# Two scalars loaded to one partition and spread by a product of ones, with the opening of the kernel reordered around them

## The chip, the cores and the metric

The kernel runs on one core of a Trainium2 chip. The metric is device time in microseconds of one execution, as the median of several runs. A core has five instruction streams that run beside each other and meet at semaphores: TensorE (PE, matrix products; its weight loads are shown apart as PEld), VectorE (DVE), ScalarE (ACT), GpSimd (POOL) and SyncE (SP, which here only issues DMA transfers). ScalarE can issue transfers too.

## The reference

Sparse attention followed by a feed-forward layer, both in float32. q, k and v have 4 batches, 8 heads, 768 positions and 64 dimensions; `n_global` is 8 and `n_local` is 96, and both come as int64 inputs.

```python
scores = q @ k.T / sqrt(D)
is_global = pos[None, :] < n_global
is_local = (rel >= 0) & (rel < n_local)          # rel = row - column
keep = is_global | is_local
dist = where(is_global & ~is_local, n_local, abs(rel))
scores = where(keep, scores - slopes * dist, -1e9)
a = softmax(scores)
x = (a @ v) in rows of 512                       # 3072 rows
h = x @ w_in                                     # 512 -> 2048
g = where(h > 0, h, exp(min(h, 0)) - 1)
out = g @ w_out                                  # 2048 -> 512
```

The two numbers are read at run time: the masks and distances of the attention depend on them.

## The kernel before, in words

The 3072 rows are worked in 12 groups of 256 rows (two tiles of 128). For each group there are four pairs of heads. A pair loads q and k together in one tile (`qk`, 312 KB) and its values in `v` and `u`; q is scaled (line 447 on ScalarE, 449 on GpSimd, 451 on VectorE), TensorE makes scores `s` (line 472), VectorE adds a table (`far0` for the first tile of a group, `far1` for the second) and takes the minimum (line 460), ScalarE takes the exponential (462), the result is divided by its sum, transposed on TensorE (525, 527), copied from PSUM to `pt` and multiplied with the values (505). The feed-forward products are lines 834 and 860 for the first four groups and 710 and 766 for the later eight. The weights come as float64 in 32 loads of 512 KB (`bits`, line 389), which VectorE, ScalarE and GpSimd turn into a high and a low float32 part (lines 391 to 410).

Nearly all of this is put in order by a planner, `Plan`, written in Python: it simulates the five engines with a cost for each operation, and gives each engine a list. Operations are picked by the earliest possible start and then by a due time; due times are counted from fixed points such as `T0` = 34 us. Three of its numbers describe the start of the program: `BW0` is the time at which transfers begin to flow, and `FREE` says when each engine is first free. They change no instruction, but move what the planner believes of the opening, and so can change which operation goes first anywhere later.

Ahead of the planned list stands `setup`, whose instructions are in the order in which they are written. It first issues the load of the two scalars from ScalarE's queue (`load_scalars`, line 228), to all 128 partitions. GpSimd writes index tables with iota, VectorE makes from them the signed distance `d`, the part of the table that doesn't depend on the scalars, and a small table `g` for the 8 global columns. When the scalars have landed, VectorE puts each together from its two 32-bit words (`scalars`, line 235) and finishes the tables: `d` becomes a mask by `n_local` (363), `g` is made of `n_global` and `n_local` (364, 366), `far0` and `far1` get the mask added (365, 367), and the global columns are put in, in `far0` by VectorE (370) and in `far1` by GpSimd (371). After that GpSimd makes the identity matrix that the transposes need, and sets small constants in the tiles `st`. From then on all engines work through the planned list.

TensorE has no work until the first scores. `warm` (line 1065 and on) fills the time with products of a tile of ones, whose result nobody reads: `COLD` = 8 of them at the start, and later, until the first feed-forward product, as many of 240 ns as the planner sees idle time for. In the trace these are `none<-fill`, line 1070.

Of the kernel before, what the change touches and what calls it, by code (L numbers as in the profile page):

```python
# [8 lines left out]
F32 = mybir.dt.float32  # L9
F32R = mybir.dt.float32r  # L10
I32 = mybir.dt.int32
AF = mybir.ActivationFunctionType
ALU = mybir.AluOpType
# [3 lines left out]
P = 128  # L17
NG = 8
# [8 lines left out]
BIG = float(2 ** 100)  # L27
# [32 lines left out]
class Plan:  # L60
# [3 lines left out]
    LAT = {"PE": 170.0, "ACT": 110.0, "DVE": 90.0, "POOL": 70.0, "SP": 1900.0}  # L64
    BW = 380.0

    BW0 = 2250.0

    FREE = {"PE": 5200.0, "ACT": 3600.0, "DVE": 5300.0, "POOL": 6000.0, "SP": 700.0}

    def __init__(self):
        self.ops = []
# [36 lines left out]
    def order(self, slots):  # L109

        free = {}
        for names in slots.values():
            for s in names:
                free[s] = 0.0
        engines = dict(self.FREE)
        port = 0.0
        bw = self.BW0
        queue = {}
# [109 lines left out]

def load_scalars(nc, pool, src):
    n = src.shape[0]  # L230
    raw = pool.tile([P, n, 2], I32, name="n_raw")
    nc.scalar.dma_start(raw, src.bitcast(I32).rearrange("(o n w) -> o n w", o=1, w=2).broadcast_to([P, n, 2]))
    return raw


def scalars(nc, pool, raw):

    n = raw.shape[1]
    up = pool.tile([P, n], F32, name="n_up")
    nc.vector.scalar_tensor_tensor(up, raw[:, :, 0], 0.0, raw[:, :, 1], ALU.is_lt, ALU.add)  # L240
    val = pool.tile([P, n], F32, name="n_val")
    nc.vector.scalar_tensor_tensor(val, up, float(2 ** 32), raw[:, :, 0], ALU.mult, ALU.add)
    return [val[:, i:i + 1] for i in range(n)]


class Kernel:
# [77 lines left out]
    def setup(self):  # L324

        nc, m = self.nc, self.m
        self.raw = load_scalars(nc, self.c, self.n_in)  # L330
        far0, far1 = self.far0.t, self.far1.t
        t = self.c.tile([P, 1], F32, name="act")
        ii = m.tile([P, LW], I32, tag="io0", name="ii")
        d = m.tile([P, LW], F32, tag="io1", name="d")
        j = self.c.tile([P, NG], I32, name="tabj")
        g = self.c.tile([P, NG], F32, name="tabg")
        after = m.tile([P, LW], F32, tag="io2", name="after")
        halves = ((slice(0, HW), BACKW + 32), (slice(HW, P), BACKW - 32))
        nc.gpsimd.memset(t, 0.0)
        nc.scalar.activation(t, t, AF.Exp)  # L340
        if self.WARM:
            self.fill = m.tile([P, 512], F32R, tag="xh2a", name="fill")
            nc.vector.memset(self.fill.bitcast(F32), 1.0)
            self.none = self.ps.tile([P, 512], F32, tag="h1", name="none")

        for r, at in halves:
            nc.gpsimd.iota(ii[r, :at + NG], pattern=[[-1, at + NG]], base=BACKW, channel_multiplier=1)
            nc.gpsimd.iota(ii[r, at + NG:], pattern=[[-1, LW - at - NG]], base=BACKW - at, channel_multiplier=1)
        nc.gpsimd.iota(j, pattern=[[1, NG]], base=0, channel_multiplier=0)
        nc.vector.tensor_copy(d, ii)  # L350
        nc.vector.tensor_scalar(after, d, 0.0, -BIG, ALU.is_lt, ALU.mult)
        nc.vector.scalar_tensor_tensor(far1, d, -1.0, after, ALU.mult, ALU.add)
        nc.scalar.copy(far0, far1)
        nc.vector.tensor_copy(g, j)
        for h in range(0, self.H, 2):
            nc.gpsimd.memset(self.scale.t[:, h // 2:h // 2 + 1], self.q_scale(h))
        nc.gpsimd.tensor_scalar(self.scale.t[HW:], self.scale.t[HW:], 2.0, 1.0, ALU.mult, ALU.mult)
        for r, at in halves:
            nc.gpsimd.memset(far0[r, :at - 32], -BIG)
            nc.gpsimd.memset(far0[r, at:at + NG], -BIG)  # L360
        self.ng, self.nl = scalars(nc, self.c, self.raw)
        ng, nl = self.ng, self.nl
        nc.vector.tensor_scalar(d, d, nl, -BIG, ALU.is_ge, ALU.mult)
        nc.vector.tensor_scalar(g, g, ng, -BIG, ALU.is_ge, ALU.mult)
        nc.vector.tensor_tensor(far0, far0, d, ALU.add)
        nc.vector.tensor_scalar(g, g, nl, None, ALU.subtract)
        nc.vector.tensor_tensor(far1, far1, d, ALU.add)
        for r, at in halves:
            x = far0[r, at - 32:at - 32 + NG]
            nc.vector.tensor_tensor(x, x, g[r], ALU.max)  # L370
            nc.gpsimd.tensor_copy(far1[r, at:at + NG], g[r])
        make_identity(nc, self.ident.t)
        if self.ON_PE:
            nc.scalar.activation(self.minus1.t, self.ident.t, AF.Copy, scale=-1.0)
        for x in self.sums.values():
            nc.gpsimd.memset(x[:, :, 1], 1e-9)


    def weight(self, which, fc, due, after):
# [608 lines left out]

    SLACK, LATER = 600.0, 3500.0

    GATE, COLD = 900.0, 8
    HINT = 40
    LOADED = 2000.0
    BACK = 3500.0
# [22 lines left out]
    def run(self):  # L1017
        self.consts()
        self.build()
        order = self.plan.order(self.slots())  # L1020
        with self.tc.manual_schedule():
            first = order[0]
            for v in first.allocs:
                v.t = v.make(v.slot)
            first.emit(first.eng)
            self.setup()
            free = self.warm(self.COLD * 240.0, 0.0)
            cold = min(op.n for op in order if op.eng == "PE" and op.allocs and op.allocs[0].cls == "h")
            last = max(i for i, op in enumerate(order) if op.eng == "PE" and op.allocs and op.allocs[0].cls == "s")
            end = max(i for i, op in enumerate(order) if op.eng == "PE")  # L1030

            self.norms = [(op.norm, op.start) for op in order if op.norm is not None and op.norm.eng == "DVE"]
            for i, op in enumerate(order):
                if op is first:
                    continue
                if op.n == cold:
                    self.WARM = False
                if op.eng == "PE" and self.WARM:

                    self.warm(op.start - free, 300.0)  # L1040
                    free = op.start + op.alts[0][1]
                for v in op.allocs:
                    v.t = v.make(v.slot)
                if op.eng == "POOL":
                    self.gate(op)
                op.emit(op.eng)
                if i == last + 40:
                    flags = self.flag()
                if i == last + 80:
                    self.flag_sum(flags)  # L1050
                if i == len(order) - self.HINT:
                    self.tc.mark_branch_hint_location("dense", hint="LikelyTaken", engines=list(mybir.ALL_ENGINES))
                if i == end:
                    flag = self.flagged()
        return flag
# [10 lines left out]
    def warm(self, ns, least):  # L1066

        nc = self.nc
        while self.WARM and ns > least:
            nc.tensor.matmul(self.none, self.fill[:, :P], self.fill, start=True, stop=True)  # L1070
            ns -= 240.0
        return self.plan.FREE["PE"]

# [225 lines left out]
```

## Time and profile before

| what | before |
|---|---|
| median of 3 runs | 644.77 us (644.61 to 646.71) |
| the profiled execution | 645.74 us, of which the span from first to last instruction is 643.9 |
| TensorE busy | 629.8 us, 98% of the span |
| VectorE busy | 495.8 us, 77% |
| ScalarE busy | 414.3 us, 64% |
| GpSimd busy | 196.9 us, 31% |
| mean granted clock of TensorE | 0.994 |
| moved by DMA | 149.82 MB, 233 GB/s |

A busy share is an average over the whole span. Stages differ, so the rows below go by stage. An instruction's row gives its start, its duration, its engine and line, output and input tiles, and in brackets how long the engine was idle before it and what ended that. "Landing" is the time from the issue of a transfer to its completion. The granted clock is 1.00 where TensorE runs at 2.4 GHz and 0.50 where it runs at 1.2 GHz.

### The profile page before, as it was taken

Reading aid. Unit: us, or ns where it says so; the run is one execution under the profiler, and the core shown is the slowest. Engines: PE = TensorE matmul, PEld = TensorE weight load, DVE = VectorE, ACT = ScalarE, POOL = GpSimd, SP = SyncE. Lnnn points to the kernel's source line nnn. Section 1 sums busy time; section 2 is a strip of 40 time slices with the busy share of each in tenths; the row PEclk is TensorE's granted clock in tenths of the full one; section 3 lists DMA queues with packets and bytes.
Section 4 is the critical chain, followed back from the end, with each engine's and each line's share of the span. In section 5 each row is a group of like instructions: output and inputs, shape, how many; then the busy total and the mean of one; then the engine's idle time right before and its main releaser. Section 6 shows DMA issues by size and latency. Waiting matters only on the chain.

```text
span 643.9 us, 19099 instructions
## 1 busy us (share of the span) xinstructions
PE 629.8 (98%) x7032; PEld 581.9 (90%) x7032; DVE 495.8 (77%) x1648; ACT 414.3 (64%) x1206; POOL 196.9 (31%) x493
## 2 busy tenths in 40 slices
PE   7989999999999999999999999999999999999995
PEld 5768888888888889999999999999999999999995
DVE  6989889888888886777767777786686776875654
ACT  6999777677554656666666576566566566555452
POOL 3546555656456662121121111112022112110000
PEclk9989999999999999999999999999999999999998
DMA  8979824322266799897879788898898898884542
GB/s 310 379 271 406 330 85 113 94 88 85 66 213 240 235 292 305 262 283 238 259 242 294 254 253 270 271 262 240 271 268 274 282 246 269 251 244 147 181 149 85
DMA packets 131171, 149.82 MB, mean 233 GB/s; under 512 B 63616, under 2 KB 82816, under 8 KB 131072
## 3 DMA queue, kind: packets, MB, share of 16 engines
q1 hardware_dynamic: 130928, 148.54, 72.6%
q8 instruction: 57, 0.93, 0.6%
q14 instruction: 42, 0.34, 0.2%
q10 hardware_dynamic: 144, 0.00, 0.0%
HBM read 117.57 MB, written 30.93 MB: 231 GB/s over the span
## 4 chain that ended last, share of the span: by engine, by line
PE 90%; DVE 3%; DMA 2%; ACT 2%; issue 1%; POOL 1%; SPq 0%; DVEq 0%; POOLq 0%; ACTq 0%
PE h L710 27%; PE o L766 24%; PE o L860 14%; PE h L834 14%; PE s L608 5%; PE s L472 4%; PE pv L505 2%; PE t L525 1%; DMA dd<-tr 1%; DMA pt<-dd 1%; DMA n_raw<-in_n_dram 1%; PE t L527 1%; DVE pr L460 1%; DVE pt L305 0%; ACT pr L462 0%
## 5 line engine op out<-in xcount | busy, mean ns | idle before, releaser
L710 PE MATMUL h<-xh,w 128*128 128x256 f32 x1024 | 142.1, 280 | 0.0
L710 PEld LDWEIGHTS h<-xh,w 128*128 128x128 f32 x1024 | 129.8, 188 | 1.9 <-issue 1.0
L720 DVE SCALAR_TENSOR_TENSOR gg<-e,h 128x256 f32<-128x256 f32 x128 | 53.3, 416 | 76.8 <-ACT e L719 76.2
L578 POOL TENSOR_SCALAR pr<-pr,st 128x168 f32<-128x168 f32 x144 | 63.0, 437 | 154.3 <-DVE st L480 141.8
L462 ACT ACTIVATE pr<-pr,nmax 128x168 f32<-128x168 f32 x192 | 82.0, 428 | 14.7 <-DVE nmax L460 12.9
L834 PEld LDWEIGHTS h<-xh,w 128*128 128x128 f32 x512 | 76.8, 188 | 10.8 <-DVE gl L311 0.8
L718 ACT ACTIVATE e<-h 128x256 f32<-128x256 f32 x128 | 48.6, 380 | 57.1 <-PE h L710 56.9
L834 PE MATMUL h<-xh,w 128*128 128x256 f32 x512 | 82.0, 283 | 0.1
L710 PE MATMUL h<-xl,w 128*128 128x256 f32 x512 | 81.8, 281 | 0.0
L860 PE MATMUL o<-w,gh 128*128 128x512 f32 x256 | 81.5, 400 | 0.0
L710 PEld LDWEIGHTS h<-xl,w 128*128 128x128 f32 x512 | 69.3, 188 | 1.9 <-issue 1.7
L460 DVE CUSTOM_DVE_ANT_0 pr<-s,far 128x168 f32<-128x168 f32 x192 | 53.4, 324 | 13.2 <-ACT xh L303 11.2
L311 POOL TENSOR_TENSOR w<-g,w 128x256 fp32r<-128x256 f32 x64 | 50.7, 813 | 38.2 <-ACT w L303 29.9
L303 ACT CAST sh<-sum 128x512 fp32r<-128x512 f32 x64 | 39.8, 622 | 31.3 <-DVE sum L734 31.3
L583 DVE STREAM_TRANSPOSE tr<-pr 128x192 f32<-128x192 f32 x144 | 50.4, 364 | 8.3 <-POOL pr L578 7.9
L719 ACT ACTIVATE e<-e 128x256 f32<-128x256 f32 x128 | 53.4, 417 | 3.6
L766 PE MATMUL o<-mix,sh 128*128 128x256 f32 x256 | 51.0, 281 | 0.0
L860 PEld LDWEIGHTS o<-w,gh 128*128 128x128 f32 x256 | 43.0, 188 | 7.6 <-issue 1.7
L311 DVE TENSOR_TENSOR sl<-sum,sh 128x512 fp32r<-128x512 f32 x64 | 44.4, 694 | 5.2 <-ACT sh L303 5.2
L766 PE MATMUL o<-w,sh 128*128 128x256 f32 x256 | 48.2, 280 | 0.0
L449 POOL TENSOR_SCALAR qk<-qk,scale 128x256 f32<-128x256 f32 x13 | 7.5, 578 | 129.9 <-DMA qk<-in_qkv_dram 84.9
L303 ACT CAST rh<-gg 128x384 fp32r<-128x384 f32 x64 | 32.8, 513 | 19.4 <-DVE gg L720 18.7
(131 smaller groups left out, 1416.7 us busy)
## 6 DMA issues: line engine op xcount, KB each, us to landing
mix<-mixed SPq DMA_DIRECT2D x192, 256.0 KB, 4.5
qk<-in_qkv_dram SPq DMA_DIRECT2D x48, 312.0 KB, 4.2
v<-in_qkv_dram SPq DMA_DIRECT2D x36, 384.0 KB, 4.8
dd<-tr SPq DMA_DIRECT2D x36, 384.0 KB, 4.4
pt<-dd SPq DMA_DIRECT2D x72, 192.0 KB, 3.9
bits<-in_w_in_dram SPq DMA_DIRECT2D x16, 512.0 KB, 7.1
bits<-in_w_out_dram SPq DMA_DIRECT2D x16, 512.0 KB, 9.5
mixed<-mix SPq DMA_DIRECT2D x32, 256.0 KB, 3.8
```

What stands on the lines that cost most here:

```text
L303: self.nc.scalar.copy(out, x)
L311: self.on(e).tensor_tensor(out, x, y, ALU.subtract)
L460: first = p.add((("DVE", 85 + 1.042 * LW, False),), lambda e: nc.vector.tensor_tensor_reduce(x(), s.t[:, i, :LW], tab, -(2.0 ** -(h + 1)), ...
L462: p.add(act(LW, extra=200), lambda e: nc.scalar.activation(x(), x(), AF.Exp, bias=nm, scale=-1.0, accum_out=st.t[:, n, 0:1]), [pr], [pr, s ...
L578: nc.gpsimd.tensor_scalar(pr.t[:, :LW], pr.t[:, :LW], st.t[:, n, 3:4], 1.0, ALU.mult, ALU.mult)
L583: nc.vector.transpose(tr.t[:, :, i, j], pr.t.rearrange("p (b r) -> p b r", r=32))
L710: nc.tensor.matmul(h.t, w1.t[:, s, cc * P:(cc + 1) * P], self.chunk(x, cc), start=n == 0 and s == HI and cc == 0, stop=n == 1 and cc == se ...
L719: p.add(act(W), lambda e: nc.scalar.activation(ex.t, ex.t, AF.Exp, scale=-1.0), [ex], [ex], d - 8000)
L720: p.add(dve(W), lambda e: nc.vector.scalar_tensor_tensor(gs(), ex.t, -1.0, h.t, ALU.add, ALU.max), [h, ex], [g], d - 8000)
L766: nc.tensor.matmul(acc[bank].t[:, half], a, b.t[:, LO if t == 1 else HI, x], start=j == 0 and t == 0 and n in first, stop=j == self.NFC // ...
L834: nc.tensor.matmul(h.t, w1.t[:, s, cc * P:(cc + 1) * P], self.chunk(x, cc), start=n == 0 and cc == 0, stop=n == 2 and cc == self.NCC - 1)
L860: nc.tensor.matmul(o.t[:, :at.stop - at.start], g.t[:, i * P:(i + 1) * P], w2.t[:, s, at], start=fc == f0 and n == 0 and s == HI, stop=fc ...
```

## The change

- The scalars are loaded to one partition instead of 128. VectorE puts them together there, TensorE multiplies them with a row of 128 ones, which gives every partition a copy in PSUM, and VectorE copies that to SBUF.
- The cast of `g` and its two steps with the scalars move from VectorE to GpSimd, the two steps now with a second operation that changes nothing (add 0).
- `make_identity` moves ahead of the table steps that need the scalars; the constants in `st` are now set before GpSimd's copies into `far1`; on VectorE the mask is added to `far1` after the global columns are put into `far0`.
- Of the opening products three stand before the product that spreads the scalars and two behind it, instead of eight in a row.
- The planner's starting numbers become smaller: transfers flow from 1.2 us on instead of 2.25, and the engines are free from 4.1 (TensorE), 3.0 (ScalarE), 4.4 (VectorE) and 4.6 us (GpSimd) instead of 5.2, 3.6, 5.3 and 6.0.

```diff
-    BW0 = 2250.0
-    FREE = {"PE": 5200.0, "ACT": 3600.0, "DVE": 5300.0, "POOL": 6000.0, "SP": 700.0}
+    BW0 = 1200.0
+    FREE = {"PE": 4100.0, "ACT": 3000.0, "DVE": 4400.0, "POOL": 4600.0, "SP": 700.0}
...
 def load_scalars(nc, pool, src):
-    raw = pool.tile([P, n, 2], I32, name="n_raw")
-    nc.scalar.dma_start(raw, src.bitcast(I32).rearrange("(o n w) -> o n w", o=1, w=2).broadcast_to([P, n, 2]))
+    raw = pool.tile([1, n, 2], I32, name="n_raw")
+    nc.scalar.dma_start(raw, src.bitcast(I32).rearrange("(o n w) -> o n w", o=1, w=2))
...
+    up = pool.tile([1, n], F32, name="n_up")
     nc.vector.scalar_tensor_tensor(up, raw[:, :, 0], 0.0, raw[:, :, 1], ALU.is_lt, ALU.add)
+    one = pool.tile([1, n], F32, name="n_one")
+    nc.vector.scalar_tensor_tensor(one, up, float(2 ** 32), raw[:, :, 0], ALU.mult, ALU.add)
+    all_ = psum.tile([P, n], F32, tag="h0", name="n_all")
+    nc.tensor.matmul(all_, ones[0:1, :P], one, start=True, stop=True)
     val = pool.tile([P, n], F32, name="n_val")
-    nc.vector.scalar_tensor_tensor(val, up, float(2 ** 32), raw[:, :, 0], ALU.mult, ALU.add)
+    nc.vector.tensor_copy(val, all_)
...
+        nc.vector.memset(ones, 1.0)
...
-        nc.vector.tensor_copy(g, j)
...
+        nc.gpsimd.tensor_copy(g, j)
...
+        make_identity(nc, self.ident.t)
+        self.warm(self.COLD[0] * 240.0, 0.0)
+        self.ng, self.nl = scalars(nc, self.c, self.raw, ones, self.ps)
+        nc.gpsimd.tensor_scalar(g, g, ng, -BIG, ALU.is_ge, ALU.mult)
+        nc.gpsimd.tensor_scalar(g, g, nl, 0.0, ALU.subtract, ALU.add)
         nc.vector.tensor_scalar(d, d, nl, -BIG, ALU.is_ge, ALU.mult)
-        nc.vector.tensor_scalar(g, g, ng, -BIG, ALU.is_ge, ALU.mult)
         nc.vector.tensor_tensor(far0, far0, d, ALU.add)
-        nc.vector.tensor_scalar(g, g, nl, None, ALU.subtract)
-        nc.vector.tensor_tensor(far1, far1, d, ALU.add)
         for r, at in halves:
             x = far0[r, at - 32:at - 32 + NG]
             nc.vector.tensor_tensor(x, x, g[r], ALU.max)
-            nc.gpsimd.tensor_copy(far1[r, at:at + NG], g[r])
-        make_identity(nc, self.ident.t)
+        nc.vector.tensor_tensor(far1, far1, d, ALU.add)
         for x in self.sums.values():
             nc.gpsimd.memset(x[:, :, 1], 1e-9)
+        for r, at in halves:
+            nc.gpsimd.tensor_copy(far1[r, at:at + NG], g[r])
...
-    GATE, COLD = 900.0, 8
+    GATE, COLD = 900.0, (3, 2)
...
-            free = self.warm(self.COLD * 240.0, 0.0)
+            free = self.warm(self.COLD[1] * 240.0, 0.0)
```

## Rows read from the trace of the kernel before

**Rows 1.** Busy time by stage: stretch, length, each engine's us (instructions), clock, DMA, GB/s
```profile
core 0: us, PE busy (x) PEld busy (x) DVE busy (x) ACT busy (x) POOL busy (x), PEclk, DMA share, GB/s
12.00:28.00 16.00, 15.31 (x224) 11.21 (x223) 15.26 (x66) 14.42 (x50) 7.09 (x14) 1.00 1.03 400
44.00:68.00 24.00, 22.59 (x279) 18.06 (x279) 22.86 (x77) 22.31 (x75) 15.87 (x22) 1.00 1.01 396
100.00:620.00 520.00, 519.64 (x5894) 490.96 (x5893) 398.24 (x1316) 323.86 (x933) 142.25 (x382) 1.00 0.74 227
```
**Rows 2.** The opening in order of time: start, duration, engine, line, operation, tiles, idle before
```profile
0.82 0.41 ACTq L232 DMA_DIRECT2D n_raw<-in_n_dram  x1
0.86 0.39 SPq L427 DMA_DIRECT2D qk<-in_qkv_dram  x1
1.54 3.59 PE L1070 MATMUL none<-fill 128*128 128x512 f32 x8 [1.54 <-DVE fill L343]
4.83 0.16 DVE L240 SCALAR_TENSOR_TENSOR n_up<-n_raw 128x2 f32<-128x2 int32 x1 [1.96 <-DMA n_raw<-in_n_dram]
5.24 0.51 ACT L447 ACTIVATE qk<-qk,scale 128x256 f32<-128x256 f32 x1 [2.09 <-DMA qk<-in_qkv_dram]
5.80 0.80 PE L472 MATMUL s<-qk 64*64 64x168 f32 x16 [0.67 <-ACT qk L447]
6.29 0.35 DVE L370 TENSOR_TENSOR far<-far,tabg 64x8 f32<-64x8 f32 x2
6.44 0.41 POOL L371 COPY far<-tabg 64x8 f32<-64x8 f32 x2 [2.83 <-DVE far L367]
6.80 0.33 DVE L460 CUSTOM_DVE_ANT_0 pr<-s,far 128x168 f32<-128x168 f32 x1
7.67 0.49 POOL L449 TENSOR_SCALAR qk<-qk,scale 128x256 f32<-128x256 f32 x1
8.21 0.80 PE L472 MATMUL s<-qk 64*64 64x168 f32 x16 [0.48 <-POOL qk L449]
8.76 0.48 POOL L449 TENSOR_SCALAR qk<-qk,scale 128x256 f32<-128x256 f32 x1 [0.60 <-DMA qk<-in_qkv_dram]
```
**Rows 3.** Transfers: packets by queue from 2.0 to 4.75, and issues (KB each, us to landing)
```profile
q1 hardware_dynamic: 185, 0.41, 54.8%
q10 hardware_dynamic: 132, 0.00, 2.2%
...
n_raw<-in_n_dram ACTq DMA_DIRECT2D x1, 2.0 KB, 4.0
qk<-in_qkv_dram SPq DMA_DIRECT2D x1, 312.0 KB, 4.3
...
qk<-in_qkv_dram SPq DMA_DIRECT2D x1, 312.0 KB, 5.0
```
**Rows 4.** Stages again: the transfers' first start, and two later starts from rest
```profile
2.13:4.50 2.37, 2.37 (x7) 1.88 (x6) 0.68 (x3) 0.94 (x3) 0.56 (x5) 1.00 0.56 137
39.00:40.50 1.50, 1.50 (x24) 1.39 (x23) 1.35 (x4) 1.19 (x4) 0.28 (x1) 1.00 0.89 219
69.75:71.50 1.75, 1.75 (x36) 1.56 (x36) 1.17 (x4) 0.99 (x2) 0.85 (x2) 1.00 0.86 194
```
**Rows 5.** Two opening products (ns min/median/max, first and last start); a stage
```profile
L1070 PE MATMUL none<-fill x2: 434/531/628, 4.3 to 4.7; 128*128 128x512 f32 x2
...
8.20:11.20 3.00, 2.99 (x36) 2.10 (x36) 1.69 (x13) 2.68 (x13) 1.64 (x4) 1.00 1.04 414
```
**Rows 6.** The dip of the clock: TensorE in order of time, and the stage
```profile
35.56 0.69 PE L525 MATMUL t<-ident,pr 128*128 128x128 f32 x2 [1.26 <-ACT pt L303]
36.60 1.40 PE L472 MATMUL s<-qk 64*64 64x168 f32 x16
...
35.50:38.60 3.10, 3.04 (x32) 2.10 (x34) 1.41 (x10) 2.32 (x10) 1.82 (x4) 0.50 0.39 147
```

More of the change, by code (lines that the diff above doesn't have):

```diff
@@ L230, in load_scalars, with scalars @@
     n = src.shape[0]
-    raw = pool.tile([P, n, 2], I32, name="n_raw")
-    nc.scalar.dma_start(raw, src.bitcast(I32).rearrange("(o n w) -> o n w", o=1, w=2).broadcast_to([P, n, 2]))
+    raw = pool.tile([1, n, 2], I32, name="n_raw")
+    nc.scalar.dma_start(raw, src.bitcast(I32).rearrange("(o n w) -> o n w", o=1, w=2))
     return raw
-def scalars(nc, pool, raw):
+def scalars(nc, pool, raw, ones, psum):
     n = raw.shape[1]
-    up = pool.tile([P, n], F32, name="n_up")
+    up = pool.tile([1, n], F32, name="n_up")
     nc.vector.scalar_tensor_tensor(up, raw[:, :, 0], 0.0, raw[:, :, 1], ALU.is_lt, ALU.add)
+    one = pool.tile([1, n], F32, name="n_one")
+    nc.vector.scalar_tensor_tensor(one, up, float(2 ** 32), raw[:, :, 0], ALU.mult, ALU.add)
+    all_ = psum.tile([P, n], F32, tag="h0", name="n_all")
+    nc.tensor.matmul(all_, ones[0:1, :P], one, start=True, stop=True)
     val = pool.tile([P, n], F32, name="n_val")
-    nc.vector.scalar_tensor_tensor(val, up, float(2 ** 32), raw[:, :, 0], ALU.mult, ALU.add)
+    nc.vector.tensor_copy(val, all_)
     return [val[:, i:i + 1] for i in range(n)]
@@ L337, in setup @@
         after = m.tile([P, LW], F32, tag="io2", name="after")
+        ones = self.c.tile([1, P], F32, name="ones")
         halves = ((slice(0, HW), BACKW + 32), (slice(HW, P), BACKW - 32))
@@ L340, in setup @@
         nc.scalar.activation(t, t, AF.Exp)
[L341 to L344, printed above, removed]
+        self.fill = m.tile([P, 512], F32R, tag="xh2a", name="fill")
+        nc.vector.memset(self.fill.bitcast(F32), 1.0)
+        self.none = self.ps.tile([P, 512], F32, tag="h1", name="none")
         for r, at in halves:
@@ L360, in setup @@
             nc.gpsimd.memset(far0[r, at:at + NG], -BIG)
-        self.ng, self.nl = scalars(nc, self.c, self.raw)
+        make_identity(nc, self.ident.t)
+        if self.ON_PE:
+            nc.scalar.activation(self.minus1.t, self.ident.t, AF.Copy, scale=-1.0)
+        self.warm(self.COLD[0] * 240.0, 0.0)
+        self.ng, self.nl = scalars(nc, self.c, self.raw, ones, self.ps)
         ng, nl = self.ng, self.nl
+        nc.gpsimd.tensor_scalar(g, g, ng, -BIG, ALU.is_ge, ALU.mult)
+        nc.gpsimd.tensor_scalar(g, g, nl, 0.0, ALU.subtract, ALU.add)
         nc.vector.tensor_scalar(d, d, nl, -BIG, ALU.is_ge, ALU.mult)
-        nc.vector.tensor_scalar(g, g, ng, -BIG, ALU.is_ge, ALU.mult)
         nc.vector.tensor_tensor(far0, far0, d, ALU.add)
-        nc.vector.tensor_scalar(g, g, nl, None, ALU.subtract)
-        nc.vector.tensor_tensor(far1, far1, d, ALU.add)
         for r, at in halves:
@@ L370, in setup @@
             nc.vector.tensor_tensor(x, x, g[r], ALU.max)
-            nc.gpsimd.tensor_copy(far1[r, at:at + NG], g[r])
-        make_identity(nc, self.ident.t)
-        if self.ON_PE:
-            nc.scalar.activation(self.minus1.t, self.ident.t, AF.Copy, scale=-1.0)
+        nc.vector.tensor_tensor(far1, far1, d, ALU.add)
         for x in self.sums.values():
             nc.gpsimd.memset(x[:, :, 1], 1e-9)
+        for r, at in halves:
+            nc.gpsimd.tensor_copy(far1[r, at:at + NG], g[r])
     def weight(self, which, fc, due, after):
```

## The prediction, made before the changed kernel ran

> **What bounds the kernel now.** I read the page's busy shares first (TensorE 629.8 us of a span of 643.9), then a table of stages, then the opening in order of time. The stages [rows 1] say where a saved microsecond counts. From 100 to 620 us TensorE is busy 519.64 of 520: that stretch is bound by TensorE, the edit adds and removes nothing in it, so it comes earlier or later as a block, and the stores at the end with it. The result is decided by when TensorE gets through the opening, before about 100 us. There, from 12 to 28 us, everything is nearly full: VectorE 15.26 of 16, ScalarE 14.42, DMA share 1.03 at 400 GB/s; from 44 to 68 it is the same (22.86 and 22.31 of 24, 396 GB/s). Such a stretch can't be hurried by one engine alone; but if loads and softmaxes both start earlier by the same amount, it is shifted whole.
>
> The opening in order of time [rows 2] has two chains. One is the scalars: issued at 0.82, used by VectorE at 4.83 after an idle of 1.96 us; then the table steps, GpSimd's copies into far1 (it was idle 2.83 us before them), its identity matrix and st memsets, its scaling of the second qk at 7.67, score products at 8.21. The other is the first qk load: issued at 0.86, scaled by ScalarE at 5.24 after an idle of 2.09 us, score products at 5.80, and the first softmax step at 6.80, which the tables and not the scores hold back: those have been there since 6.6. The landing times are 4.0 us for the scalars and 4.3 for qk [rows 3].
>
> **The scalar load.** Before, it is 2 KB to 128 partitions; its queue shows 132 packets between 2.0 and 4.75 us beside 185 of the main queue [rows 3]. From 2.13 to 4.5 us the engines moved 137 GB/s x 2.37 us = 325 KB at a share of only 0.56 [rows 4]. Twice later the transfers start from rest with no such load beside them: 219 GB/s over the first 1.5 us at 39.0, 194 over 1.75 us at 69.75. The same 325 KB take 1.48 or 1.68 us at these rates, 0.89 or 0.69 us less than 2.37. I read that as small and large packets being fed to the same engines in turn. Bounds for what the removal gives the first qk: 0 (every start from rest is slow, and the small packets cost nothing) and 1.56 us (325 KB at the 400 GB/s of the full stretch take 0.81). I take 0.9, the restart at 39.0, the nearer one in size of transfer: a qk load again. The Trainium skill (DMA: Bandwidth & Descriptors, "HWDGE ordering") says that SP's and ScalarE's queues each have one ring on the same 16 engines and no descriptor generator of their own. By that rule the small packets do cost the large ones, and the term stands near 0.9; two independent queues would put it at 0. The shares of rows 3 and 4 side with the rule without proving it.
>
> The scalars' own landing lies between 2.1 us (the stretch of rows 4 begins at 2.13 with the first packet of the main queue, 1.27 us after its issue, and a single small packet has nothing behind it) and 4.8 as now. VectorE comes to the first scalar step only when its earlier steps are done, now at 4.83 - 1.96 = 2.87; the cast of g leaves it there and a memset of ones comes in, so about 2.9. I take "landed by then"; one packet is far from 132.
>
> **The spread.** Two one-partition steps (0.16 each, as n_up now), a product with two columns (between nothing and the 0.63 of an opening product at the low clock [rows 5]; I take 0.4), a copy from PSUM (0.16 again), three hand-overs of 0.05, like the one from ScalarE's end at 5.75 to the scores at 5.80: 2.9 + 0.32 + 0.4 + 0.16 + 0.15 = 3.9 us for n_val, against 5.2 now (4.83 and two steps). If the scalars land no earlier, it is 5.9, 0.7 late. From n_val the table steps now run until 6.64, 1.4 us; two of them, the steps on g, go to GpSimd (0.2 each, as its copies of the same size) and run beside d and far0: about 1.2 is left, so tables at 5.1.
>
> **GpSimd.** Identity and st memsets fill 0.82 us between the far1 copies (end 6.85) and the scaling at 7.67. Both go ahead of the copies, the identity ahead of the wait for n_val too, into the idle of 2.83 us, and are hidden; if that idle is gone, they cost their 0.82 again. Behind the new wait for n_val stand the g steps, memsets, far1 copies (0.41) and all scalings of qk. Copies end at 5.1 + 0.05 + 0.41 = 5.6. The second qk was issued at 2.24 and took 5.0 us to land [rows 3]: 7.24 now, 6.35 with 0.9 off. So the load, not GpSimd, is then last: second scores at 6.35 + 0.49 + 0.05 = 6.9 instead of 8.21. The third qk, for which GpSimd waits already (8.76), comes 0.9 earlier.
>
> **The opening products.** Eight in a row become three, the small product, and two. With the first qk at 4.35, ScalarE's 0.51 and a hand-over put the scores at 4.9. Eight take 3.59 us, so three end near 2.9; the spread's product runs by 3.7 and two more end by 4.6: they don't hold up the scores, and cost 0 on the path. If the scalars land at 4.8, they do, to about 6.5.
>
> **Sum.** First scores 5.80 to 4.9, second 1.3 earlier, third qk 0.9 earlier: the smallest, 0.9, goes into the full stretch at 12 us, since DMA is full there as well. The profiled execution took 645.74 (the span and 1.84 around it), 0.97 above the median: 645.74 - 0.9 = 644.8 for it, and 644.77 - 0.9 = 643.9 for the median. The planner's lower start times (BW0 by 1.05 us, TensorE by 1.1, GpSimd by 1.4) also change which operation is issued next, and how many planned products fill gaps. No row prices that; I take 0, with ends of 1.5 us either way, the largest single disturbance of the opening, which comes next.
>
> **Rivals.** (1) *A dip of the clock goes too.* At 34.3 TensorE sits idle 1.26 us for a ScalarE copy, and from 35.5 to 38.6 the granted clock is 0.50, 1.2 GHz [rows 6]: 16 score products take 1.40 us instead of 0.80. TensorE is busy 3.04 of these 3.1 us, work for 1.5 at the full clock. The dip hangs on one wait, and the order changes; but ScalarE, for which it waits, stays nearly full, so a wait can come back anywhere. Time 643.9 - 1.5 = 642.4.
>
> (2) *The earlier start is not earlier.* If the slow start is the transfers' own, qk keeps its 4.3 us, only the tables gain, and the full DMA stretch takes that back: 644.8. The restart at 69.75, with 0.69, speaks half for it.
>
> (3) *Slower, by the clock.* Of the opening products the one at 4.3 takes 0.63 us and the last, at 4.7, 0.43 [rows 5]: the clock rises from 1.2 to 2.4 GHz there, 3.2 us after the first of them at 1.54, with unbroken products before it, and ahead of the first scores. After the edit there are gaps near 3.0 and 3.5. If the level stays low through the first scores, the stretch from 8.2 to 11.2, now 2.99 of 3 us busy [rows 5] and on the chain, takes longer: twice as long at worst, +3.0; if the clock rises 3.2 us after the scores begin, about +1.2 for two groups of scores (0.60 each). With 0.9 off that is 645.1 to 646.9; I take 645.9. It decides if the first 16 score products last 1.4 us rather than 0.8. For it speaks the pause; against it, that each pause is under 0.6 us. The Trainium skill (TensorE: Matmul & The Clock Gate, "What's actually happening") says that the low level is the state of rest and that activity releases it. The opening rows agree, and by that rule cutting eight products to five is a risk that the diff does not show.
>
> **How the numbers follow.** Forecast 643.9 with 0.45 (own range 643.2 to 644.6: the shift between 0.2 and 1.56); dip gone, 642.4, with 0.27; no shift, 644.8, with 0.13; clock, 645.9, with 0.15. About 0.3%, 1.9 us, is what a measurement here can tell from no change, so faster is under 642.84 and slower over 646.7. Faster: most of the dip case (0.22) and 0.08 of the forecast with a luckier order, 0.30. Slower: a third of the clock case and an unlucky order, 0.08. Same: 0.62. The range 641.8 to 646.1 leaves out dip cases with an extra gain and the worse half of the clock case, about 0.15.
>
> **What would show it.** Right: VectorE has no wait for the scalars; ScalarE's first scaling near 4.35, first scores near 4.9, first softmax step near 5.5 (now 6.80), second scores near 6.9, loads of the first 28 us about 0.9 earlier; and the stretch from 100 to 620 us unchanged but early. Wrong: the first scaling still at 5.2; score groups of 1.4 us in the opening; another stretch at 0.50, or none, between 28 and 68 us; a gain at 12 us that is gone at 100.

## The result and the profile after

| | before | after |
|---|---|---|
| median, runs side by side (21 each) | 645.61 us (644.61 to 648.38) | 648.76 us (646.58 to 656.66) |
| ratio after/before, 95% interval | | 1.0057 [1.0043, 1.0071] |
| the profiled execution | 645.74, span 643.9 | 649.79, span 648.0 |
| TensorE busy, granted clock | 629.8 us, 0.994 | 632.7 us, 0.997 |

The changed kernel is slower: by 3.1 us between the medians, by 0.57% or 3.7 us in the ratio, where 0.9 us of gain was forecast and 646.1 was the upper end. (The execution of 656.66 us, at a granted clock of 0.989, counts as slow and is not in the ratio; the two medians alone would give 1.0049.) The profiled execution lies 1.0 us above its median. The forecast of 643.9 was counted from 644.77, the median of three runs; over 21 runs the kernel before takes 645.61, so 0.8 of the 4.9 us between 643.9 and 648.76 lay in the base.

The opening of the changed kernel in order of time, columns as in [rows 2]:

```profile
0.83 0.52 ACTq L232 DMA_DIRECT2D n_raw<-in_n_dram  x1
0.86 0.39 SPq L433 DMA_DIRECT2D qk<-in_qkv_dram  x1
1.54 1.65 PE L1076 MATMUL none<-fill 128*128 128x512 f32 x3 [1.54 <-DVE fill L347]
2.72 0.14 DVE L240 SCALAR_TENSOR_TENSOR n_up<-n_raw 1x2 f32<-1x2 int32 x1
3.12 0.58 PE L244 MATMUL n_all<-n_one,ones 1*128 1x2 f32 x2
3.74 0.16 DVE L246 COPY n_val<-n_all 128x2 f32<-128x2 f32 x1 [0.70 <-PE n_all L244]
3.88 0.51 ACT L453 ACTIVATE qk<-qk,scale 128x256 f32<-128x256 f32 x1 [0.71 <-DMA qk<-in_qkv_dram]
4.79 1.40 PE L478 MATMUL s<-qk 64*64 64x168 f32 x16
5.78 0.33 DVE L466 CUSTOM_DVE_ANT_0 pr<-s,far 128x168 f32<-128x168 f32 x1
6.12 2.07 PE L1076 MATMUL none<-fill 128*128 128x512 f32 x4
6.90 0.48 POOL L455 TENSOR_SCALAR qk<-qk,scale 128x256 f32<-128x256 f32 x1 [0.46 <-DMA qk<-in_qkv_dram]
8.12 1.26 PE L478 MATMUL s<-qk 64*64 64x168 f32 x16
9.31 0.96 PE L1076 MATMUL none<-fill 128*128 128x512 f32 x3
```

The same opening, its landing times and its transfer stage, columns as in [rows 3] and [rows 4]:

```profile
qk<-in_qkv_dram SPq DMA_DIRECT2D x1, 312.0 KB, 2.9
...
qk<-in_qkv_dram SPq DMA_DIRECT2D x1, 312.0 KB, 4.5
...
2.13:4.50 2.37, 2.37 (x7) 1.33 (x5) 1.44 (x8) 1.53 (x4) 1.40 (x9) 1.00 0.96 334
```

The edits do in the opening what they say, and more: VectorE no longer waits for the scalars, the first qk lands after 2.9 us instead of 4.3, the transfers run at 334 GB/s where they ran at 137, and the first scores start at 4.79 instead of 5.80. But 16 score products now take 1.40 us, which in [rows 6] is their time at 1.2 GHz, against 0.80 in [rows 2]. Four idle-time products that the planner put behind them take 2.07 us at that level, and the second scores come at 8.12, 0.1 earlier than before instead of 1.3. The first scores waited for such products too: ScalarE's scaling ended at 4.39 (3.88 + 0.51), while the two opening products behind the spreading one ran from 3.64 to 4.86. (The clock column of the stage reads 1.00 here, as in [rows 4], so the level is read from the durations: the products that start at 9.31 take the 0.32 us each of the higher level.)

Stages of the changed kernel, columns as in [rows 1]:

```profile
12.00:28.00 16.00, 15.80 (x226) 11.62 (x226) 15.05 (x67) 14.96 (x52) 6.06 (x13) 1.00 1.04 400
35.50:38.60 3.10, 2.39 (x40) 1.77 (x37) 3.00 (x12) 3.10 (x13) 3.10 (x5) 1.00 0.62 189
44.00:68.00 24.00, 22.31 (x273) 18.29 (x269) 21.80 (x77) 21.16 (x72) 15.91 (x22) 1.00 0.99 386
68.00:177.00 109.00, 108.50 (x968) 95.49 (x964) 93.44 (x244) 72.71 (x197) 58.19 (x104) 1.00 0.37 116
177.00:260.00 83.00, 80.10 (x730) 69.65 (x719) 65.07 (x186) 45.95 (x144) 44.99 (x89) 1.00 0.74 241
100.00:620.00 520.00, 516.26 (x5857) 486.42 (x5856) 394.89 (x1308) 322.12 (x927) 139.95 (x380) 1.00 0.73 226
```

Two stages of the kernel before, not among its rows above:

```profile
68.00:177.00 109.00, 108.97 (x979) 96.00 (x980) 94.58 (x238) 74.93 (x202) 62.87 (x106) 1.00 0.37 116
177.00:260.00 83.00, 83.00 (x765) 73.69 (x754) 66.97 (x196) 48.64 (x150) 44.66 (x90) 1.00 0.82 256
```

The dip of the clock at 35.5 is gone. From 12 to 28 TensorE is fuller (15.80 against 15.31), in part with products that nobody reads, of which the planner now places 21 against 14 (26 and 22 in all, less 5 and 8 of the opening). From 44 to 68 and from 68 to 177 it is idle 1.69 and 0.50 us, against 1.41 and 0.03 before. The block of which the prediction said that the edit "adds and removes nothing in it" has changed: from 100 to 620 us TensorE is idle 3.74 us (520 - 516.26) instead of 0.36, and 2.90 of them (83.00 - 80.10) lie between 177 and 260, where before it was never idle. TensorE's waits there in the changed kernel (us in total, times, longest):

```profile
PE o L866 <- ACT gh L307: 1.3, 2, 0.9
PE h L840 <- DVE gl L315: 0.8, 1, 0.8
PE s L614 <- DMA pt<-dd: 0.7, 1, 0.7
```

And ScalarE and TensorE around the first of these, in order of time:

```profile
185.35 0.41 ACT L307 CAST mix<-tf 128x256 fp32r<-128x256 f32 x1 [2.01 <-DMA mixed<-mix]
185.66 0.37 ACT L307 CAST gh<-h 128x256 fp32r<-128x256 f32 x1
...
189.69 0.37 ACT L307 CAST gh<-h 128x256 fp32r<-128x256 f32 x1 [1.97 <-DVE h L848]
190.12 0.73 PE L866 MATMUL o<-w,gh 128*128 128x512 f32 x2 [0.94 <-ACT gh L307]
```

These steps belong to the preparation of the later groups' weights (`mix`, stored to `mixed`), which the planner spreads among the first four groups' products. A cast into a `mix` buffer waits 2.01 us until an earlier content of the buffer has been stored; behind it in ScalarE's list stand casts of `gh`, an operand of the product `o`. (The `gh` at 189.69, for which TensorE waits, had itself waited 1.97 us for VectorE, so that the store is behind TensorE's wait is a conjecture here; the buffers further down test it.) The last product of the first four groups closes this work, and its start is a landmark (the line's view: ns of one as min/median/max, first and last start), here of the changed kernel:

```profile
L866 PE MATMUL o<-w,gl x128: 390/394/505, 39.6 to 258.4; 128*128 128x512 f32 x128
```

and of the kernel before:

```profile
L860 PE MATMUL o<-w,gl x128: 388/394/499, 40.6 to 254.3; 128*128 128x512 f32 x128
```

It is 4.1 us later, although the first of them came 1.0 earlier. From there to the last product of the kernel it is 382.4 us in the one and 382.3 in the other (to 640.8 and 636.6). So the loss of this execution is complete at 258 us. It also begins late: the 82nd of these 128 products starts at the same time in both, first before, then after:

```profile
182.73 0.39 PE L860 MATMUL o<-w,gl 128*128 128x512 f32 x1
182.73 0.39 PE L866 MATMUL o<-w,gl 128*128 128x512 f32 x1
```

From this product to the last one stand 670 products in both kernels, as many of each kind. In the kernel before no two neighbours of them start more than 0.42 us apart. In the changed kernel five pairs do (0.54, 1.34, 1.17, 0.89 and 0.77 us, near 186, 190, 211, 242 and 250), and these five take 3.8 us more than such neighbours usually do, of the 4.1. The 2.90 us of idle time are less, because a product is shown as 0.39 us long where the next one usually starts 0.23 us behind it, so that a part of each wait lies under the shown product.

### The profile page after: what moved, and what is told of

Same layout as the page of the kernel before. It is cut to its first block, busy times and chain, and to the rows that moved or that the text cites. A ratio compares the mean times of both kernels' runs of the same rounds, so it can differ in the third digit from the quotient of the medians.

```text
span 648.0 us, 19100 instructions
## 1 busy us (share of the span) xinstructions
PE 632.7 (98%) x7038; PEld 583.0 (90%) x7038; DVE 497.0 (77%) x1657; ACT 412.4 (64%) x1202; POOL 193.4 (30%) x490
## 3 DMA queue, kind: packets, MB, share of 16 engines
q1 hardware_dynamic: 130928, 148.54, 71.6%
## 4 chain that ended last, share of the span: by engine, by line
PE 81%; DVE 6%; DMA 5%; ACT 3%; issue 2%; POOL 1%; SPq 0%; DVEq 0%; POOLq 0%; ACTq 0%
PE h L716 27%; PE o L772 24%; PE o L866 10%; PE h L840 10%; PE s L614 4%; PE s L478 3%; DMA qk<-in_qkv_dram 2%; DMA mixed<-mix 1%; DMA bits<-in_w_out_dram 1%; PE pv L511 1%; DMA bits<-in_w_in_dram 1%; DVE pr L466 1%; ACT pr L468 1%; DVE mix L315 1%; DVE h L848 1%
## 5 line engine op out<-in xcount | busy, mean ns | idle before, releaser
L726 DVE SCALAR_TENSOR_TENSOR gg<-e,h 128x256 f32<-128x256 f32 x128 | 53.3, 416 | 75.9 <-ACT e L725 75.3
L315 POOL TENSOR_TENSOR w<-g,w 128x256 fp32r<-128x256 f32 x64 | 48.1, 776 | 42.0 <-ACT w L307 23.4
L866 PE MATMUL o<-w,gl 128*128 128x512 f32 x128 | 45.1, 399 | 0.0
```

The source lines that it names most:

```text
L315: self.on(e).tensor_tensor(out, x, y, ALU.subtract)
L726: p.add(dve(W), lambda e: nc.vector.scalar_tensor_tensor(gs(), ex.t, -1.0, h.t, ALU.add, ALU.max), [h, ex], [g], d - 8000)
L866: nc.tensor.matmul(o.t[:, :at.stop - at.start], g.t[:, i * P:(i + 1) * P], w2.t[:, s, at], start=fc == f0 and n == 0 and s == HI, stop=fc ...
```

## The experiments

No edited instruction runs after 7 us, so the theory was that the planner's new numbers (`BW0`, `FREE`) give another order of the same work, and that this order costs the time. "Order" stands here for all that the planner decides. It is more than the sequence, and that the numbers "change no instruction" is not so: for many operations the planner also picks the engine. The instruction counts of the kernel before, with its own numbers and then with the new ones, differ by 7 products on TensorE (those that nobody reads), 10 more on VectorE, 4 fewer on ScalarE and 6 fewer on GpSimd:

```profile
PE 629.8 (98%) x7032; PEld 581.9 (90%) x7032; DVE 495.8 (77%) x1648; ACT 414.3 (64%) x1206; POOL 196.9 (31%) x493
PE 634.4 (98%) x7039; PEld 585.1 (90%) x7039; DVE 497.3 (76%) x1658; ACT 412.2 (63%) x1202; POOL 190.6 (29%) x487
```

No run here tells the sequence from the choice of engines. The rival was the opening's clock: five products in two parts leave TensorE at 1.2 GHz through the first scores. Times are medians; each ratio is to the kernel before in runs on the same chip (median 645.4 to 646.5 throughout), with its 95% interval.

**The numbers alone.** The first kernel is the changed one with the planner's numbers of before, the second the kernel before with the changed numbers.

```diff
-    BW0 = 1200.0
-    FREE = {"PE": 4100.0, "ACT": 3000.0, "DVE": 4400.0, "POOL": 4600.0, "SP": 700.0}
+    BW0 = 2250.0
+    FREE = {"PE": 5200.0, "ACT": 3600.0, "DVE": 5300.0, "POOL": 6000.0, "SP": 700.0}
```

> The changed kernel with the planner's starting numbers of before (BW0 and FREE), so that the planned order is that of before and only the opening's instructions differ. Theory O (the order that follows from the planner's numbers costs the time: products wait between 180 and 260 us behind the weight mixing): within 1 us of the kernel before, 644.6 to 646.6, and TensorE idle for under 0.8 us between 100 and 620 us. Theory C (the low clock in the opening and the edits themselves cost it): about 3 us slower than before, 648 to 649, with the loss in place before 100 us.

> The kernel before with the changed planner numbers alone; scalars, identity and opening products are as before. Theory O: about 3 us slower than before, 648 to 649, TensorE idle for over 2 us between 100 and 620 us. Theory C: within 1 us of before.

Measured: all edits with the old numbers 645.57 us, 1.0000 [0.9979, 1.0021]; the new numbers without the edits 650.40 us, 1.0063 [1.0040, 1.0086]. So the planner's new numbers make the loss, with the edits and without them, and the edits by themselves make no difference that can be measured (1.4 us or more would have shown). The stage from 177 to 260 us, first with all edits and the old numbers:

```profile
177.00:260.00 83.00, 83.00 (x758) 73.92 (x756) 66.69 (x194) 48.86 (x150) 44.55 (x90) 1.00 0.82 258
```

then the kernel before with the new numbers:

```profile
177.00:260.00 83.00, 80.57 (x775) 69.92 (x774) 65.25 (x185) 44.96 (x142) 45.12 (x89) 1.00 0.72 231
```

The idle time goes with the numbers: 0 with the old, 2.43 us with the new. Whether the edits with the old numbers have the forecast gain isn't shown. In the profiled execution their last `o<-w,gl` starts at 253.5, 0.8 before that of the kernel before, but four executions in this order differ by 2.2 us there (table below). This one lost the 0.8 again late, at one wait and a dip of the clock (TensorE in order of time, then the stage):

```profile
413.45 0.48 PE L772 MATMUL o<-mix,sh 128*128 128x256 f32 x2 [1.93 <-DMA mix<-mixed]
...
413.80:417.20 3.40, 3.40 (x19) 3.40 (x18) 0.84 (x2) 0.12 (x1) 0.00 (x0) 0.51 0.97 341
```

A gain of 0.8 us is below what the times can tell.

**The opening's clock.** Five products before the spreading one instead of three, in the changed kernel and in the one with the old numbers:

```diff
-    GATE, COLD = 900.0, (3, 2)
+    GATE, COLD = 900.0, (5, 2)
```

> The changed kernel with five opening products ahead of the spread instead of three (two behind it as it is), so that TensorE has no pause until the first scores. Both theories: the granted clock rises near 4.8 us instead of 9.1, the first 16 score products take 0.8 us instead of 1.4, the second group of scores starts near 7.4 instead of 8.1. Theory C: the whole gains 2 us or more over the changed kernel. Theory O: it gains under 1 us, since the stalls after 180 us stay.

> Both together: planner numbers of before and five opening products ahead of the spread. Theory O: faster than the kernel before by about the 0.9 us that the prediction gave the earlier start, 644 to 645. Theory C: the same, so this run tells them apart only by e1 beside it: under C it is 2 us faster than e1, under O by under 1 us.

Measured: 651.10 us, 1.0079 [1.0054, 1.0105], and 645.86 us, 1.0001 [0.9982, 1.0019]. No gain in either. In the profile of the first the edit did not do what it was for: the first scores still took 1.40 us. The rival falls by the first two kernels instead: all edits with the old numbers have first scores of 1.40 us and no loss, and the kernel before with the new numbers, whose opening has eight products in a row and first scores of 0.92 us, has all of it. One execution at either level also shows that five products don't set the level for certain. TensorE in order of time, in the changed kernel with five:

```profile
5.64 1.40 PE L478 MATMUL s<-qk 64*64 64x168 f32 x16
```

and with the old numbers and five:

```profile
5.57 0.80 PE L478 MATMUL s<-qk 64*64 64x168 f32 x16
```

The five opening products take 2.50 us from 1.54 on in both. It is the same seven products and the spreading one between them, and the first scores ran at 1.2 GHz in one and at 2.4 in the other. By the durations of single products the level rose at 9.6 us and at 5.4. In both the scores came later than the 4.79 of the changed kernel, although ScalarE's scaling began at 3.87 and 3.85: the products that nobody reads stood in their way.

**Each number alone**, in the changed kernel: `BW0` of before with the new `FREE`, and the new `BW0` with `FREE` of before (half of the first diff each).

> The changed kernel with the transfers' start of before (BW0 2.25 us) and the engines' new start times. If the stalls follow from transfers that the planner believes to be earlier: 645 to 646. If they follow from the engines' start times: 648 to 649. If any change of order has its own luck, anything between 644 and 651, with another place of the idle time.

> The changed kernel with the engines' start times of before and the changed start of the transfers alone. BW0 restored alone gave 645.2. If the transfers' start makes the bad order: 648 or more. If only the two together make it: 645 to 646.5. In the profile the places of idle TensorE between 177 and 260 us say whether it is the same trouble.

Measured: 645.20 us, 0.9990 [0.9973, 1.0008], and 646.22 us, 1.0008 [0.9990, 1.0025]. By these medians either number of before takes the loss away, and it takes both to make it. The profiles are less clear. With `BW0` of before TensorE is idle 0.10 us between 177 and 260. With `FREE` of before it is idle 1.67 us there, behind the same waits for `gh` and `dd`, and its last `o<-w,gl` starts at 258.0; that execution, of 648.18 us, was the slowest of its twelve. So this third order has the same trouble at least at times, and why its median is 2 us lower isn't shown.

**The planner's due points moved along** with the earlier start, by 1.1 us:

```diff
-    T0, STEP0, STEP, LEAD, NE = 34000.0, 3000.0, 3000.0, (4000.0, 12000.0), 3
+    T0, STEP0, STEP, LEAD, NE = 32900.0, 3000.0, 3000.0, (4000.0, 12000.0), 3
-    PREPARE, SE = (168000.0, 9000.0, 6000.0), 4
+    PREPARE, SE = (166900.0, 9000.0, 6000.0), 4
```

> The changed kernel with the planner's fixed due points moved along by 1.1 us (T0 32.9 and the start of the mixing 166.9 us). If the loss came from due points that were left behind when the start moved: the idle time between 177 and 260 us falls below 1 us and the time to 645 to 646. If not: it stays at 648 or more, or changes place.

Measured: 647.29 us, 1.0017 [0.9997, 1.0038], with 0.96 us of idle TensorE between 177 and 260 (83.00 - 82.04) in the profiled execution. Some of the loss may be back: the interval ends below the 1.0043 at which that of the changed kernel begins in the first comparison, but at the 1.0038 at which it begins in the second, and the changed kernel was not timed beside it. The idle time fell below 1 us, as the theory had it; the time did not fall to 646. That the due points are a part of the matter isn't shown: they too give another order.

**More buffers, same order.** If the wait of ScalarE's cast for a stored buffer is what costs, a free buffer for it must help. In the preparation between 167 and 232 us a `mix` tile may take one of two idle buffers (`io2`, `io3`), or in the second kernel of up to eight; the order on every engine stays as it was. (`left` counts the uses still to come of what lies in a buffer, `gone` is the planned end of its last use.) The two buffers are also tried with all the old numbers, the eight with the old `BW0`.

```diff
+    if v in self.owned and 167000 < op.start < 232000:
+        can = [s for s in (v.slot, "io2", "io3") if not left.get(seat.get(s), 0)]
+        v.slot = min(can, key=lambda s: gone.get(s, 0.0))
```

> The changed kernel, every engine's instructions in the same order, but the mixing of weights (the tiles mix of prepare) may also use two buffers that are idle from 166 to 244 us (io2, io3), so that it waits less for the landing of its own stores. Theory M (ScalarE's cast into a mix buffer waits for a store, and the cast gh that TensorE needs stands behind it in ScalarE's queue): TensorE's idle time between 177 and 260 us falls from 2.9 us to under 1, and the time falls by about 2 us, to 646 to 647 where before is at 645.6. Rival V (VectorE, full with the mixing, is late by itself): idle time and time stay as in the changed kernel, 648.5 to 649.5.

> The changed kernel in its own order, with up to eight more idle buffers for the mixing. Theory M (the wait for buffers whose stores have not landed, on ScalarE, with gh behind it): no wait of ScalarE for a store between 177 and 260 us, no idle TensorE near 190 and 250, and 1 to 2 us less than the changed kernel beside it. Rival V (VectorE's own order): the idle time near 210 (0.8 us, which had VectorE's gl before it with two buffers more) stays, and the time falls by under 1 us. Both can hold in part: then 0.5 to 1.5 us less, with 210 left.

> The same two buffers with the planner numbers of before (so with the order of before and the changed opening). That order has no idle time between 177 and 260 us to win back. Theory M: within 0.5 us of the changed opening in the order of before, 645 to 646. If it is faster by 1 us or more, the order of before also loses to these waits in executions that no profile has shown.

> A candidate to beat both: the changed opening with the transfers' start of before, whose order showed 0.1 us of idle time between 177 and 260 us, and more buffers for the mixing. If the mixing's waits cost time in executions that the one profile does not show: 644 to 645, under before by 0.2% or more. If not: as without the buffers, 645.2, which no interval here tells from before.

Measured: with two buffers 648.95 us, 1.0048 [1.0025, 1.0071] (1.44 us of idle time between 177 and 260); with up to eight 648.86, 1.0068 [1.0042, 1.0095]; with two and the old numbers 646.18, 1.0008 [0.9990, 1.0026]; with up to eight and the old `BW0` 645.93, 1.0006 [0.9984, 1.0027]. In the profile of the kernel with eight, ScalarE waits for no store between 177 and 260 us, and the wait of 0.94 us at 190 is gone. The stage and TensorE's waits in it:

```profile
177.00:260.00 83.00, 81.84 (x751) 71.67 (x742) 66.96 (x191) 47.44 (x148) 45.05 (x89) 1.00 0.76 247
...
PE h L842 <- DVE gl L316: 0.8, 1, 0.8
PE o L868 <- ACT gh L308: 0.4, 1, 0.4
```

The idle time is 1.16 us instead of 2.90, and yet the median does not move. The wait for VectorE's `gl` stays, as rival V said it would; that VectorE is late by its own list was not tested. That profile was of the fastest of that kernel's executions (646.96), so it was profiled again, and the changed kernel too.

**The same kernels again**: the changed kernel timed once more, and two further profiled executions of each of the kernel with eight buffers and the changed kernel, with no further edit.

> The changed kernel as it is, measured beside the next three on one chip. Both theories: some 3 us slower than before, ratio 1.004 to 1.007, and in the profile the same places of idle TensorE (near 190, 211 and 250 us).

> Another profiled execution of the changed kernel with eight more buffers for the mixing, whose first profile (645.2 us of span) was of its fastest execution. If its typical time of 648.9 comes from the stage of the mixing after all: TensorE idle for over 2 us between 177 and 260 us here. If it comes from elsewhere (a fall of the clock, the opening): idle for about 1.2 us there, as in the first profile, and the excess in another stage.

> A third profiled execution of the same kernel, with the same two expectations.

> A third profiled execution of the changed kernel. Idle between 177 and 260 us was 2.9 and 1.8 in the first two; if this stage makes the difference to the kernel with more buffers, it is at least 1.8 again, 0.6 us or more above that kernel's.

> A fourth profiled execution of the changed kernel, with the same expectation.

Measured: the changed kernel again 649.02 us, 1.0054 [1.0038, 1.0070]; the single profiled executions 650.68 and 650.28 (eight buffers), 648.36 and 649.21 (changed kernel). The idle time from 177 to 260 is 2.90, 1.80, 1.88 and 1.66 us in four executions of the changed kernel; with eight buffers it is 1.16, 1.39 and 2.67. In the execution with 2.67, two waits for another transfer take the place of the removed one:

```profile
PE s L615 <- DMA pt<-dd: 1.4, 2, 1.1
```

In the other the clock fell at 47 us, behind a wait of the new order (TensorE in order of time, then the stage, which has 0.52 of the clock):

```profile
47.76 1.64 PE L479 MATMUL s<-qk 64*64 64x168 f32 x16 [1.07 <-DVE nmax L467]
...
47.00:54.00 7.00, 6.24 (x36) 5.02 (x38) 5.52 (x22) 4.50 (x15) 4.59 (x5) 0.52 1.03 408
```

The start of the last `o<-w,gl`, in all profiles with the two orders (us):

| order | executions | mean |
|---|---|---|
| of before | 254.3 (before), 253.5, 255.2 (five products), 253.0 (two buffers) | 254.0 |
| new, changed kernel as it is | 258.4, 258.8, 256.9, 257.8 | 258.0 |
| new, with two buffers | 256.6 | |
| new, with eight buffers | 256.6, 259.7, 257.8 | 258.0 |
| new, other openings | 258.8 (five products), 260.9 (opening of before) | |

The two orders don't overlap: 253.0 to 255.2 against 256.6 to 260.9. The first two means differ by 4.0 us, the medians of the kernels before and after by 3.1 and 3.6 in the two comparisons. So the loss is in the first 258 us. The start of the 82nd of these products, and the time from it to the last, with 670 products between them in all profiles, as many of each kind, say where (us, executions as above):

| order | 82nd | from there to the last |
|---|---|---|
| of before | 182.7, 182.0, 183.6, 181.2 | 71.6, 71.6, 71.6, 71.8 |
| new, changed kernel as it is | 182.7, 184.5, 182.5, 183.7 | 75.7, 74.3, 74.4, 74.1 |
| new, with two buffers | 182.7 | 73.8 |
| new, with eight buffers | 183.0, 185.9, 182.6 | 73.6, 73.8, 75.2 |
| new, other openings | 183.5, 185.6 | 75.3, 75.3 |

Up to the 82nd the orders overlap, and the first two means differ by 1.0 us. Behind it they differ by 3.0, and every execution in the new order is 1.8 us or more above every one in that of before. With eight buffers this stretch is 0.4 us shorter than in the changed kernel on the mean, and still some 2 us or more too long: in the first of the three, two of the five late starts are left, near 210 and 248 (1.16 and 0.77 us from one product to the next), which wait for VectorE's `gl` and ScalarE's `gh`. So the buffer wait is a part of the loss in some executions; taking it away doesn't take the loss away. No version was faster than the kernel before: the lowest ratio of all, 0.9990, has 1 in its interval.

## Why the prediction was wrong

**What bounds the kernel.** Right that the end follows from when TensorE gets through the first part, and that the later part is a block. Wrong where the block begins. It was put at 100 us because [rows 1] show TensorE full from there; but that is full in the order of before, and the planner orders everything up to about 258 us.

**The failed step** is "The planner's lower start times ... No row prices that; I take 0, with ends of 1.5 us either way". It measured 4.7 us (650.40 - 645.68) with the opening of before, and 3.1 in the median of the changed kernel, net of what its opening gained. In its place the runs show that the planner, from the new numbers, orders the work so that TensorE waits for casts of ScalarE and VectorE and for the transfers `pt<-dd`: 1.7 to 2.9 us of idle time between 177 and 260, where all four profiles with the order of before have none, and 0.5 to 0.6 between 68 and 177 against 0.0. Of the 4.0 us by which the changed kernel is late at 258 on the mean of four executions, 3.0 arise behind the 82nd `o<-w,gl`; the 1.0 ahead of it, with the wait at 47 us and the clock, differs from one execution to the next. The step also left out that the numbers choose the engine of some operations. Which displaced or moved operation makes the order a bad one stays open.

**The scalar load.** Right in direction, undersized. 0.9 was taken, the first qk came 1.4 sooner, near the upper bound of 1.56. This start reached 334 GB/s, so the full stretch was the better row for it than the restart at 39.0 in [rows 4]. That it follows from the opening's edits and not from the planner's numbers is seen in the first two kernels of the experiments: with the edits and the old numbers ScalarE's first scaling begins at 3.85, with the new numbers alone at 5.24 as before. The second qk gained 0.5 (5.0 to 4.5). The Trainium skill (DMA: Bandwidth & Descriptors, "HWDGE ordering") speaks of rings on the same engines for both queues; the trace agrees, with the 1.4 us beside it.

**The opening products** were put at "cost 0 on the path". They cost some: the first scores could have followed ScalarE's scaling at 4.44 (4.39 and a hand-over) and started at 4.79, behind the two products at the low level. That this is near the forecast 4.9 is luck: the load came 0.5 sooner than the 4.35 that was forecast for the scaling, and these products ate most of it.

**The spread and GpSimd.** n_val was there at 3.90, as worked out (3.9), but by two errors that cancel: the scalars had landed before 2.72, where 2.9 was taken, and the product took 0.58 where 0.4 was taken. First softmax step at 5.78 (forecast 5.5). The tables were late for it, by GpSimd. Its identity matrix, which the prediction had hidden, was not quite: it ends later than n_val comes, and the two steps on g behind it take 0.33 us each where 0.2 was taken. VectorE waits 0.32 us for them. GpSimd in order of time there in the changed kernel, and VectorE's step that waited:

```profile
3.98 0.29 POOL masks.py:199 TENSOR_SCALAR_AFFINE_SELECT ident<-ident 128x128 f32<-128x128 f32 x1
4.36 0.33 POOL L371 TENSOR_SCALAR tabg<-tabg,n_val 128x8 f32<-128x8 f32 x1
4.79 0.34 POOL L372 TENSOR_SCALAR tabg<-tabg,n_val 128x8 f32<-128x8 f32 x1
...
5.16 0.34 DVE L377 TENSOR_TENSOR far<-far,tabg 64x8 f32<-64x8 f32 x2 [0.32 <-POOL tabg L372]
```

"The load, not GpSimd, is then last" held for the second qk: GpSimd's scaling ends at 7.38, with 0.46 of idle time ahead of it that the load ended. But its scores came at 8.12 and not at 6.9: the load came 0.5 sooner instead of 0.9, and then TensorE was still in the four planned products at the low level.

**Rival 3, the clock.** Its condition came true in the profile (1.40 us and not 0.8), and it ate most of the opening's gain there. It does not explain the result: with the same opening, first scores of 1.40 us and the old numbers, the time is that of before.

**Rival 1, the dip.** It went, as described, and "a wait can come back anywhere" is what happened: the new order has TensorE wait 1.06 us at 46.4, and in two of four executions of the changed kernel the clock then falls: the granted clock from 46 to 54 us is 0.79 in these and 1.00 in the other two. With the order of before the dip at 35 shows in three of four profiles.

**Rival 2** (no earlier start) fell: the qk load is earlier.

**The chances.** Slower had 0.08, from the clock and "an unlucky order". The order is the largest unknown of this change and should have had ends of some 5 us and a rival of its own, as "the planner's order is worse in the first 258 us". A row hinted at it: in [rows 1], from 44 to 68, TensorE, VectorE, ScalarE and the transfers are nearly full at once, so another order may well leave one of them waiting. Most of the loss then came elsewhere, behind 182 us.

## What to carry to other kernels

Where an edit changes the numbers from which a scheduler orders the work, the order is a term of its own, and the widest one: the same work under another plan cost 3 us here, more than every local term of the sum. Run the edit with the old numbers and the old code with the new numbers before believing either; a gain of 0.8 us in an opening can't be seen behind that. To find where two orders part, compare the start of the same product in both, the 82nd of a kind for instance: idle time alone showed 2.9 of 4.1 us. A stage in which one engine is full is full only in the order in which it was measured.

## What the runs showed of the hardware

- A 2 KB load to 128 partitions (132 packets in [rows 3]) on a second queue held a 312 KB load back by 1.4 us (4.3 to 2.9), and halved the rate of that stretch and more (334 to 137 GB/s). The two kernels with the numbers exchanged agree: 326 GB/s with the edits, 130 without.
- The start of the higher clock level differs between executions of the same instructions. By single durations it rises at 9.1 and 10.1 us in two executions of the changed kernel and at 7.7 and 7.0 in two more, and with the seven-product opening at 9.6 and 5.4. One profile of an opening can't tell when its clock rises.
- A dip to 0.50 of the clock follows the same wait in some executions and not in others: behind the 1.06 or 1.07 us that TensorE waits near 47 us in the new order, the granted clock from 46 to 54 is 1.00 in two executions of the changed kernel, 0.79 in two, and 0.58 in one with eight buffers. One came in the middle of dense products, at 413.8 us, behind a wait of 1.93 us.
